# Decode attention and FFN over cached keys: the last batch's values in freed key slots, batches 0 to 6 finished while it loads

## The chip, the cores and the metric

The kernel runs on one core of one Trainium2 chip. The metric is the device time of one execution in microseconds (us); of several runs the median is taken.

The core has five engines with instruction queues of their own: TensorE (PE in the profile; PEld is its weight load), VectorE (DVE), ScalarE (ACT), GpSimd (POOL) and SyncE (SP). Here SP computes nothing: it issues all transfers (DMAs), in the order of its own instructions, and an issue that must wait for a semaphore holds up those behind it.

## The reference

Two layers of attention and two of a dense FFN, alternating, for 8 batches of one token each. Both attention layers read the same key and value caches and the same weights, and so do both FFN layers.

```
x: [8, 1, 512]   k_cache, v_cache: [8, 8, 8192, 128]   wq: [512, 4096]   wo: [4096, 512]
w1: [512, 1792]  w2: [1792, 512]    all bf16
def A(x):   q = (x @ wq) in 32 heads of 128; 4 heads share one of 8 key/value groups
            p = softmax(q . k / sqrt(128)) over 8192 keys;  o = p . v;  return o @ wo
def B(x):   return silu(x @ w1) @ w2
x = x + A(layernorm(x)); x = x + B(layernorm(x))
x = x + A(layernorm(x)); x = x + B(layernorm(x))
```

A batch's second attention needs its own first attention and first FFN; batches do not depend on each other. Each (batch, group) has 2 MB of keys and 2 MB of values, 256 MB in all.

## The kernel before, in words

A *unit* is (layer, batch, group): scores of 4 heads against 8192 keys, a softmax, and the product with the values. There are 128 units. Keys are loaded once for both layers: batch b's eight key blocks are kept in eight *slots* (`kts`, 2 MB each), turned in place by VectorE (L694, four transposes a block), used by layer 0 and later by layer 1. Values are loaded twice, once for each layer.

The work is cut in passes, `for b in range(-1, NB)`. Pass b holds layer 1 of batch b and layer 0 of batch b + 1, woven together by `pass_of`: a slot is given to batch b + 1's keys as soon as batch b's second use of it is scored (`scored[g]`). Pass -1 has only layer 0 of batch 0, pass 7 only layer 1 of batch 7. Between passes stands the turn: the output projection sum (`x2_node`), the FFN of one batch (`ffn_nodes`), a second norm, and the queries of groups 0 to 3 (`queries_0`, L642, weights resident). To have transfers to hide the turn, the value work of the last four layer-1 units of a pass is held back (`held`) and done after it: 16 single cells.

Values, wq's second half (`queries_1`, L665) and layer 0's wo pass through a *ring* of 7 cells of 512 KB. A load takes one cell or two neighbouring ones (`cells=1` or `2`), and waits on SP until the value product (L842) or projection that last read the cells is done. `values(h, wo, cells)` makes one unit's value work: loads, four value products of 8 matmuls each, then a high part by ScalarE (L852), a low part by VectorE (L856), a gather by TensorE (L864). In layer 0 the unit's wo block is loaded between its values (before the third quarter, or before the fourth with single cells) and multiplied at once (L915). In layer 1 the normed result goes to `qab` (L874).

In pass 7, wq's second half is asked for by the unit of group 4 (L1026), behind the values of groups 0 and 1, which are in the load order by then. All of wo for layer 1 is loaded once (`load_wo_all`, two loads of 2 MB to slots 0 and 2) after five units' values. At the end `out_proj_b` (L933) multiplies one group at a time for all 8 batches, then one FFN for all 8 (`ffn_nodes("e", big, 0, NB, ...)`: norm statistics L422, squares L436 and L440, six matmuls for each batch; the power L457 on GpSimd; up L492; tanh L498; gate L502; down L510), a turn to rows (L1058), a copy and the store.

The order on each engine is not written by hand. Every piece of work is a node with an engine, an estimated duration, a priority and its dependencies. `Plan.run` plays them through, with all loads strictly in the order in which they were made, and emits the instructions in the order in which that play started them. What it assumes: `RATE` us per MB of a load by its number of cells, `LAND` us from the end of a load's transfer to its use, a factor `PE_SLOW` on TensorE's durations. It also picks the ring cell of each load. These numbers set only the order and the cells; correctness comes from semaphores that `Sync` places.

Of the kernel before, what the change touches and what calls it, by code (L numbers as in the profile page):

```python
# [14 lines left out]
N_P = 3  # L15
# [120 lines left out]
class Plan:  # L136
# [4 lines left out]
    LAND = 2.0  # L141
    HOP = 0.1
    PE_SLOW = 1.15
# [107 lines left out]
def _build(ctx, nc, A_x, A_k_cache, A_v_cache, A_wq, A_wo, B_w1, B_w2, out):  # L251
# [68 lines left out]
    wsem = {n: DmaCounter(syn.new_sem(f"w_{n}")) for n in ("w1", "w2", "x", "wq0")}  # L320
# [89 lines left out]
    def norm_nodes(tag, prio, b0, nb, deps):  # L410
# [49 lines left out]
        def apply():  # L460
            if nb == 1:
                op(dve, lambda: dve.tensor_scalar(
                    xn[:, b0, :], xs[:, b0, :], nm, rstd[:, 0:1], op0=ALU.add, op1=ALU.mult),
                    reads=[res("xs"), res("misc"), res("rstd")], writes=[res("xn")])
            else:
                nmb = nm.unsqueeze(2).to_broadcast([128, nb, KT])
                rs = rstd[:, 0:nb].unsqueeze(2).to_broadcast([128, nb, KT])
                op(dve, lambda: dve.tensor_tensor(big_x, xs[:, bs, :], nmb, ALU.add),
                   reads=[res("xs"), res("misc")], writes=[res("ring", 1)])
                op(dve, lambda: dve.tensor_tensor(xn[:, bs, :], big_x, rs, ALU.mult),  # L470
                   reads=[res("ring", 1), res("rstd")], writes=[res("xn")])
# [9 lines left out]
    def ffn_nodes(tag, prio, b0, nb, deps):  # L481
# [3 lines left out]
        th, hs = (th1[:, :], hs1[:, :]) if nb == 1 else (big_th, big_hs)  # L485
# [212 lines left out]
    def keys(layer, b, g, q_dep, late=None, first=False):  # L698
# [5 lines left out]
        if late is None:  # L704
            sm = plain[0] % N_P
            plain[0] += 1
        else:
            sm = N_P + late
# [29 lines left out]
        for q in range(4):  # L738
# [11 lines left out]
            sn.append(plan.add(f"s{u}.{q}", "PE", 0.3, score, pr - 1,  # L750
# [68 lines left out]
    def values(h, wo=None, cells=2):  # L819

        layer, b, g, u, sm = h["layer"], h["b"], h["g"], h["u"], h["sm"]
        pr = count[0] - 1
# [5 lines left out]
        for P in range(4):  # L828
            if P == (2 if cells == 2 else 3) and wo is not None:
                h["wo"] = load_wo(wo)  # L830
            if P % cells == 0:
                vn = load_v(b, g, P, cells)

            def pv(P=P, vn=vn):


                vt = gran(vn.give, cells).rearrange("p (a c t n) -> p a c t n", a=cells, c=2, t=4)[:, P % cells]
                steps = []
                for c in range(2):
                    for t in range(4):  # L840
                        k = 32 * (2 * P + c) + 8 * t
                        steps.append(lambda t=t, c=c, k=k: pe.matmul(  # L842
                            ot[32 * t:32 * t + 2 * R, 0:2 * DH], pt[:, k:k + 2 * R], vt[:, c, t],
                            start=(P == 0 and c == 0), stop=(P == 3 and c == 1)))
                mms(steps, reads=cells_of(vn) + [res("p", sm)], writes=[res("ot", o)], add=(P > 0))
            n = plan.add(f"v{u}.{P}", "PE", 0.35, pv, pr, [h["exp"], vn, old or clear_n] + vs[-1:])
            if P % cells == cells - 1:
                frees(n, vn)
            vs.append(n)

# [73 lines left out]
    def out_proj_b(h, wn, prev):  # L924

        g = h["g"]

        def mul():
            w = slot(2 * (g // 4)).rearrange("p (h d) -> p h d", h=16)
            steps = []  # L930
            for r in range(R):
                for dt in range(KT):
                    steps.append(lambda r=r, dt=dt: pe.matmul(  # L933
                        YT[:, dt * NB:(dt + 1) * NB], w[:, R * (g % 4) + r, dt * 128:(dt + 1) * 128],
                        qab[:, :, R * g + r],
                        start=(g == 0 and r == 0 and dt == 0), stop=(g == G - 1 and r == R - 1),
                        skip_group_check=True))
            mms(steps, reads=[res("wo_all", g // 4)] + [res("attnb", g, b) for b in range(NB)],
                writes=[res("yt")], add=g > 0)
        return plan.add(f"e.w{g}", "PE", 0.56, mul, count[0] - 3, [h["n"], wn, prev])  # L940
# [25 lines left out]

    wo_all = []
    def load_wo_all():
        for i in range(2):
            n = plan.load(f"woall{i}", 4, None, scored[2 * i], ring=False)  # L970

            def emit(i=i):
                dma(sp, slot(2 * i).rearrange("p (h d) -> p h d", h=16), wo_v[:, 16 * i:16 * i + 16, :], ksem[2 * i],
                    writes=[res("kt", 2 * i), res("wo_all", i)])

            n.emit = emit
            wo_all.append(n)
# [19 lines left out]
    for b in range(-1, NB):  # L997
        ready = None
        prio = FIRST
        if b >= 0:  # L1000
# [5 lines left out]
            for h in held:  # L1006
                values(h, cells=1)
                ends.append(h)
        ks, vs, held_units = pass_of(b)
# [3 lines left out]
        def advance(unit):  # L1013
            while unit not in made:
                k = todo.pop(0)
                layer, kb, g = k
                if layer == 0:
# [4 lines left out]
                    if kb == 0 and g == 4:  # L1022
                        first_q.update(queries_1("f", count[0] - 5, 0, NB, [f5]))
                    made[k] = keys(0, kb, g, first_q[g])
                else:
                    if g == 4:  # L1026
                        second_q.update(queries_1(f"c{b}", count[0] - 3, b, 1, [ready]))
                    made[k] = keys(1, kb, g, second_q[g], held_units.index(k) if k in held_units else None, g == 0)

        for i, v in enumerate(vs):  # L1030
            advance(vs[min(i + (1 if i == 0 and b >= 0 else 2), len(vs) - 1)])
            if b == NB - 1 and i == 5:
                load_wo_all()
            if v[0] == 0:
                a_values(made[v], cells=1 if b >= 0 and i >= len(vs) - 3 else 2)
# [7 lines left out]

    w = free_yt[0]
    for h in ends[-G:]:
        w = out_proj_b(h, wo_all[h["g"] // 4], w)

    def e_x2():
        op(dve, lambda: dve.tensor_tensor(
            xs[:, :, :], YT[:, 0:KT * NB].rearrange("p (k b) -> p b k", b=NB), xs[:, :, :], ALU.add),  # L1050
            reads=[res("yt"), res("xs")], writes=[res("xs")])

    big = count[0] + 10
    n = plan.add("e.x2", "DVE", 0.2, e_x2, big, [w])
    n = ffn_nodes("e", big, 0, NB, [n])
# [54 lines left out]
```

## Time and profile before

| | |
|---|---|
| median of 5 runs | 1185.18 us (1183.28 to 1187.04) |
| profiled execution, its own time | 1187.04 us |
| its span, first to last instruction | 1185.3 us |
| mean granted TensorE clock | 0.67 |
| TensorE busy, VectorE busy | 709.1 us (60%), 596.8 us (50%) |
| ScalarE busy, GpSimd busy | 136.9 us (12%), 117.3 us (10%) |
| moved by DMA | 467.13 MB, mean 394 GB/s |
| SP waiting for value products (L842) | 653.8 us in 298 waits |
| SP waiting for scores (L746) | 156.4 us in 29 waits |

The page comes from one execution, the slowest of the five. Busy times are shares of the whole span. A table of windows gives the same by stretch: for each stretch its limits, its length, busy time and number of instructions of PE, PEld, DVE, ACT and POOL, the granted TensorE clock, the mean busy share of the 16 DMA engines and the GB/s moved. A timeline line gives the start, the duration, the engine, the line and the tiles, and in brackets how long the engine was idle before it and what ended that. A chain of waits gives a start, a length and what the end of the program hung on in that time.

### The profile page before, as it was taken

How to read it: one execution, taken by the hardware profiler on the slowest of the kernel's cores; microseconds unless marked ns; L12 is line 12 of the kernel's file. 1: busy time of each engine (PE TensorE's matmuls, PEld its weight loads, DVE VectorE, ACT ScalarE, POOL GpSimd, SP SyncE). 2: the span in 40 equal slices, each digit the busy share in tenths (PEclk: the TensorE clock that was granted, in tenths of full speed). 3: DMA queues.
4: the chain of work that ended last, by engine and by line, in shares of the span. 5: the costliest groups of instructions: out<-in, count | busy, mean ns of one | idle time of the engine just before them, and what ended most of it. 6: DMA issues, size and time to landing. Idle time of an engine off the chain costs nothing.

```text
span 1185.3 us, 31675 instructions
## 1 busy us (share of the span) xinstructions
PE 709.1 (60%) x13588; PEld 370.4 (31%) x13588; DVE 596.8 (50%) x1713; ACT 136.9 (12%) x475; POOL 117.3 (10%) x295
## 2 busy tenths in 40 slices
PE   2544555675565855656665756658556575566754
PEld 1222332342332423323332333324233242332433
DVE  5652367625565255733557245752557426563321
ACT  0010011111111110110111111111101111111110
POOL 1000011100110000100111000110101001110110
PEclk8565677656665576766767576775768667675775
DMA  9999799999999999999999999999999999999994
GB/s 364 422 420 347 310 421 420 411 404 400 415 412 378 404 374 415 425 405 386 419 423 408 407 400 415 413 406 398 411 406 414 406 382 422 408 399 389 384 349 174
DMA packets 86413, 467.13 MB, mean 394 GB/s; under 512 B 8944, under 2 KB 14848, under 8 KB 61952
## 3 DMA queue, kind: packets, MB, share of 16 engines
q1 hardware_dynamic: 86272, 465.10, 97.7%
q8 instruction: 107, 1.75, 0.6%
q14 instruction: 34, 0.28, 0.1%
HBM read 465.05 MB, written 0.01 MB: 392 GB/s over the span
## 4 chain that ended last, share of the span: by engine, by line
DMA 78%; PE 16%; issue 4%; DVE 1%; SPq 1%; POOLq 0%; ACT 0%; POOL 0%; DVEq 0%; ACTq 0%
DMA ring<-in_A_v_cache_dram 73%; PE ot L842 7%; PE sc L746 5%; DMA ring<-in_A_wq_dram 2%; DMA w<-in_B_w_dram 1%; DMA kts<-in_A_k_cache_dram 1%; PE misc L642 1%; SPq L340 1%; DVE kts L694 0%; PE ex L864 0%; PE sc L721 0%; PE yt L915 0%; PE misc L510 0%; DVE small L758 0%; PE ex L886 0%
## 5 line engine op out<-in xcount | busy, mean ns | idle before, releaser
L842 PE MATMUL ot<-ring,p 128*8 128x256 bf16 x4096 | 256.7, 364 | 223.0 <-DMA ring<-in_A_v_cache_dram 221.0
L694 DVE STREAM_TRANSPOSE kts<-kts 128x1024 uint32<-128x1024 uint32 x256 | 306.0, 1221 | 40.7 <-DMA kts<-in_A_k_cache_dram 40.6
L746 PE MATMUL sc<-kts,bd 128*32 128x256 bf16 x4096 | 288.3, 406 | 30.1 <-DVE kts L694 18.6
L842 PEld LDWEIGHTS ot<-ring,p 128*8 128x8 bf16 x4096 | 80.6, 92 | 316.6 <-DMA ring<-in_A_v_cache_dram 292.2
L746 PEld LDWEIGHTS sc<-kts,bd 128*32 128x32 bf16 x4096 | 115.0, 117 | 104.6 <-DVE kts L694 28.1
L856 DVE TENSOR_TENSOR part<-ot,p 128x256 bf16<-128x256 f32 x128 | 54.2, 424 | 171.2 <-ACT p L852 97.1
L763 POOL PARTITION_ALL_REDUCE small<-small x128 | 47.8, 373 | 640.4 <-DVE small L759 395.9
L772 ACT ACTIVATE expd<-sc,small 128x256 bf16<-128x256 f32 x128 | 60.7, 474 | 425.2 <-DVE small L767 376.5
L852 ACT ACTIVATE p<-ot 128x256 bf16<-128x256 f32 x128 | 49.0, 383 | 488.6 <-PE ot L842 487.6
L778 PE MATMUL sc<-expd,ident 128*32 128x256 bf16 x512 | 42.6, 322 | 91.5 <-ACT expd L772 88.0
L758 DVE TENSOR_REDUCE small<-sc 128x1 f32<-128x256 f32 x128 | 53.2, 416 | 54.4 <-PE sc L746 54.3
L792 POOL PARTITION_ALL_REDUCE small<-small x128 | 55.3, 432 | 217.6 <-DVE small L788 217.6
L729 DVE TENSOR_TENSOR bd<-sc,mask 128x64 bf16<-128x64 f32 x128 | 27.8, 217 | 82.9 <-PE sc L746 73.8
L785 DVE STREAM_TRANSPOSE p<-sc 128x256 bf16<-128x256 bf16 x128 | 56.9, 444 | 8.0 <-PE sc L778 5.9
L778 PEld LDWEIGHTS sc<-expd,ident 128*32 128x32 bf16 x512 | 15.3, 109 | 123.6 <-ACT expd L772 121.4
L788 DVE TENSOR_SCALAR small<-hm,small 128x4 f32<-128x4 f32 x128 | 26.4, 207 | 33.3 <-ACT expd L772 33.2
L864 PE MATMUL ex<-diag,p 128*128 128x4 bf16 x256 | 26.4, 172 | 23.8 <-DVE part L856 22.4
L915 PE MATMUL yt<-z,ring 128*128 128x4 bf16 x1024 | 36.1, 166 | 6.3 <-DVE z L893 4.7
L915 PEld LDWEIGHTS yt<-z,ring 128*128 128x128 bf16 x1024 | 31.3, 100 | 26.6 <-issue 25.9
L864 PEld LDWEIGHTS ex<-diag,p 128*128 128x128 bf16 x256 | 16.5, 105 | 72.9 <-issue 38.7
L767 DVE SCALAR_TENSOR_TENSOR small<-small,hm 128x4 f32<-128x4 f32 x128 | 19.4, 152 | 36.0 <-POOL small L763 36.0
L759 DVE TENSOR_SCALAR small<-hneg,small 128x4 f32<-128x4 f32 x128 | 29.4, 230 | 4.5
(82 smaller groups left out, 434.7 us busy)
## 6 DMA issues: line engine op xcount, KB each, us to landing
ring<-in_A_v_cache_dram SPq DMA_DIRECT2D x260, 512.0 KB, 8.2
kts<-in_A_k_cache_dram SPq DMA_DIRECT2D x64, 2048.0 KB, 11.4
ring<-in_A_v_cache_dram SPq DMA_DIRECT2D x126, 1024.0 KB, 11.0
ring<-in_A_wo_dram SPq DMA_DIRECT2D x64, 512.0 KB, 11.4
ring<-in_A_wq_dram SPq DMA_DIRECT2D x36, 512.0 KB, 9.8
kts<-in_A_wo_dram SPq DMA_DIRECT2D x2, 2048.0 KB, 15.6
w<-in_B_w_dram SPq DMA_DIRECT2D x2, 1792.0 KB, 14.2
wq<-in_A_wq_dram SPq DMA_DIRECT2D x4, 512.0 KB, 11.2
```

What stands on the lines that cost most here:

```text
L694: op(dve, lambda: dve.transpose(v, v), reads=[], writes=[res("kt", g)], add=(q > 0))
L746: steps.append(lambda t=t, y=y, w=w: pe.matmul(sc[32 * t:32 * t + 32, 0:256], w, kv[:, 2 * t + y, q], start=(q == 0 and y == 0), stop=(q = ...
L758: op(dve, lambda: dve.tensor_reduce(mxr[si], sv, AX.X, ALU.max), reads=[res(*scr)], writes=[res("mxr", si)])
L763: op(pool, lambda: pool.partition_all_reduce(mxa[si], mxp[si], 128, bass.bass_isa.ReduceOp.max), reads=[res("mxp", si)], writes=[res("mxa" ...
L772: op(act, lambda: act.activation(pe_out[:, :], sv, ACT.Exp, bias=bias[si], scale=SM_SCALE, accum_out=rsum[si]), reads=[res(*scr), res("bia ...
L778: steps = [lambda P=P: pe.matmul(sc[32 * P:32 * P + 32, 256:512], src[:, P], pe_out[:, :], start=True, stop=True) for P in range(4)]
L785: op(dve, lambda: dve.transpose(pt[:, :], src), reads=[res(*scr)], writes=[res("p", sm)])
L792: op(pool, lambda: pool.partition_all_reduce(ssa[si], ssm[si], 128, bass.bass_isa.ReduceOp.add), reads=[res("mxp", si)], writes=[res("mxa" ...
L842: steps.append(lambda t=t, c=c, k=k: pe.matmul(ot[32 * t:32 * t + 2 * R, 0:2 * DH], pt[:, k:k + 2 * R], vt[:, c, t], start=(P == 0 and c = ...
L852: op(act, lambda: act.activation(pt[:, :], ot[:, 0:2 * DH], ACT.Copy), reads=[res("ot", o)], writes=[res("p", sm)])
L856: op(dve, lambda: dve.tensor_tensor(part[:, :], ot[:, 0:2 * DH], pt[:, :], ALU.subtract), reads=[res("ot", o), res("p", sm)], writes=[res( ...
L915: steps.append(lambda j=j, dt=dt: pe.matmul(YT[:, dt * R:(dt + 1) * R], w[:, j, dt * 128:(dt + 1) * 128], zt[:, R * j:R * j + R], start=(g ...
```

## The change

Six edits:

1. The last batch's pass is taken out of the loop and written out. wq's second half is asked for right behind the held values of batch 6. The keys' work of groups 0 to 6 is made at once, each with a buffer of its own for its probabilities (`buf`); group 7 uses group 0's again, after its values. Groups 0 and 1 load values through the ring in single cells, groups 2 to 7 into key slots 0, 1, 2, 5, 6, 7 by `load_v_slot`, each when the slot is scored; group 7's in three loads of 2, 1 and 1 quarters. wo goes to slots 3 and 4, between group 4's and group 5's values.
2. The second output projection, residual sum and FFN are made twice: for batches 0 to 6 ("d") while the last batch loads, and for batch 7 alone ("e") at the end. Scratch tiles are cut to the number of batches.
3. Layer 0's wo block is loaded behind all of its unit's values.
4. The last three layer-0 units of pass -1 also load single cells, as those of the other passes do.
5. The planner's numbers: `LAND` 2.0 to 5.0, `PE_SLOW` 1.15 to 1.0, a score node 0.3 to 0.45, a value node 0.35 to 0.4.
6. `queries_1` also depends on the copy of the first half's queries; three more semaphores.

```diff
-    LAND = 2.0
+    LAND = 5.0
...
-    PE_SLOW = 1.15
+    PE_SLOW = 1.0
...
+    def load_v_slot(b, g, k):
+        parts = (2, 1, 1) if g == G - 1 else (4,)
+        src = A_v_cache[b, g].rearrange("(p y) d -> p (y d)", p=128)
+        got = []
+        for i, cells in enumerate(parts):
+            q = sum(parts[:i])
+            where = res("vs", k, i)
+
+            def emit(i=i, q=q, cells=cells, where=where):
+                dma(sp, slot(k)[:, GR * q:GR * (q + cells)], src[:, GR * q:GR * (q + cells)],
+                    ksem[k] if len(parts) == 1 else wsem[f"end{i}"],
+                    writes=[where] + ([res("kt", k)] if i == 0 else []))
+
+            n = plan.load(f"v{b}.{g}.{q}", cells, emit, scored[k], ring=False)
+            got += [(n, slot(k)[:, GR * (q + j):GR * (q + j + 1)], where) for j in range(cells)]
+        return got
...
-        pr = count[0] - 1
+        pr = count[0] - 1 if b < NB - 1 else u + 1
+        quarters = load_v_slot(b, g, at) if at is not None else None
...
-            if P == (2 if cells == 2 else 3) and wo is not None:
-                h["wo"] = load_wo(wo)
-            if P % cells == 0:
+            if quarters:
+                vn = quarters[P][0]
+            elif P % cells == 0:
                 vn = load_v(b, g, P, cells)
...
+        if wo is not None:
+            h["wo"] = load_wo(wo)
...
-                a_values(made[v], cells=1 if b >= 0 and i >= len(vs) - 3 else 2)
+                a_values(made[v], cells=1 if i >= len(vs) - 3 else 2)
...
+    fin = NB - 1
+    second_q.update(queries_1(f"c{fin}", FIRST + 6, fin, 1, [ready, second_q[3]]))
+    made = [keys(1, fin, g, second_q[g], first=g == 0, buf=g % (N_P + N_DEF)) for g in range(G - 1)]
+    values(made[0], cells=1)
+    made.append(keys(1, fin, G - 1, second_q[G - 1], buf=0))
+    values(made[1], cells=1)
+    for g, k in ((2, 0), (3, 1), (4, 2)):
+        values(made[g], at=k)
+    load_wo_all()
+    for g, k in ((5, 5), (6, 6), (7, 7)):
+        values(made[g], at=k)
     w = free_yt[0]
-    for h in ends[-G:]:
-        w = out_proj_b(h, wo_all[h["g"] // 4], w)
+    done = [h["n"] for h in ends] + [made[1]["n"]]
+    for g in range(G):
+        w = out_proj_b("d", g, 0, fin, [w, wo_all[g // 4]] + done)
+    n = x2_of("d", 0, fin, count[0] + 20, [w])
+    fed = ffn_nodes("d", count[0] + 20, 0, fin, [n, second_q[G - 1]])
+    w = n
+    for g in range(G):
+        w = out_proj_b("e", g, fin, 1, [made[g]["n"], w])
     big = count[0] + 10
-    n = plan.add("e.x2", "DVE", 0.2, e_x2, big, [w])
-    n = ffn_nodes("e", big, 0, NB, [n])
+    n = x2_of("e", fin, 1, big, [w])
+    n = ffn_nodes("e", big, fin, 1, [n, fed])
```

## The prediction

> **What bounds the kernel now.** I read the page first: the DMA row of its second part and the GB/s row under it.
>
> ```profile
> DMA  9999799999999999999999999999999999999994
> GB/s 364 422 420 347 310 421 420 411 404 400 415 412 378 404 374 415 425 405 386 419 423 408 407 400 415 413 406 398 411 406 414 406 382 422 408 399 389 384 349 174
> ```
>
> Thirty-eight slices of forty are full; TensorE is busy 60%, VectorE 50%. The kernel streams 467.13 MB, and both kernels read the same tensors once. Nothing on an engine counts unless it empties the DMA queues or lies after the last transfer. So the next view is the table of windows, 4 us each, over the places that are not full (the last two columns are DMA share and GB/s).
>
> ```profile
> 88.00:92.00 4.00, 1.03 (x16) 0.38 (x16) 4.00 (x4) 0.00 (x0) 0.00 (x0) 0.55 0.84 347
> 92.00:96.00 4.00, 3.01 (x48) 1.33 (x48) 1.06 (x4) 0.38 (x1) 0.33 (x1) 0.60 0.95 337
> 96.00:100.00 4.00, 1.88 (x48) 1.26 (x48) 1.27 (x8) 0.74 (x3) 0.47 (x2) 0.83 0.87 306
> 100.00:104.00 4.00, 1.27 (x20) 0.57 (x20) 0.42 (x1) 0.39 (x2) 0.00 (x0) 0.50 0.89 330
> ...
> 124.00:128.00 4.00, 3.63 (x96) 2.84 (x100) 0.61 (x4) 0.00 (x0) 0.00 (x0) 0.50 0.03 11
> 128.00:132.00 4.00, 2.98 (x56) 1.26 (x44) 1.81 (x10) 0.57 (x2) 0.83 (x2) 0.83 0.59 168
> ...
> 1124.00:1128.00 4.00, 2.99 (x68) 2.02 (x72) 0.50 (x3) 0.00 (x0) 0.00 (x0) 0.50 0.85 295
> 1128.00:1132.00 4.00, 3.67 (x80) 2.19 (x72) 1.19 (x6) 0.67 (x3) 0.37 (x1) 0.82 0.49 141
> ...
> 1168.00:1172.00 4.00, 2.23 (x44) 0.99 (x40) 0.42 (x1) 0.38 (x1) 0.00 (x0) 0.50 0.10 41
> ```
>
> Four holes: the end of the first pass (88 to 104), the turn after it (120 to 132), the last pass (1124 to 1132), and everything after about 1168. In between, seven windows of 140 us show shares of 1.00 to 1.02.
>
> What makes the third hole, from the chain of waits:
>
> ```profile
> 1115.29 9.84 DMA ring<-in_A_wq_dram
> 1125.17 0.60 PE misc L665 x16
> ...
> 1126.61 1.09 PE sc L746 x16
> ```
>
> The second half of wq, needed for heads groups 4 to 7 of the last batch, is asked for only behind the values of units 0 and 1. Units 4 to 7 cannot be scored before 1126, so the ring cells holding their values are not freed, and the SP queue waits. What follows the last landing, from the timeline:
>
> ```profile
> 1170.00 1.03 PE L842 MATMUL ot<-ring,p 128*8 128x256 bf16 x16 [0.80 <-DMA ring<-in_A_v_cache_dram]
> 1173.26 0.19 DVE L1049 TENSOR_TENSOR xs<-yt,xs 128x32 bf16<-128x32 f32 x1 [0.69 <-PE yt L933]
> 1175.91 1.69 POOL L457 TENSOR_TENSOR rstd<-var,expo 128x8 f32<-128x8 f32 x1 [33.20 <-DVE ring L468]
> 1177.95 1.65 PE L492 MATMUL misc<-xn,w 128*128 128x8 bf16 x56 [2.74 <-DVE xn L470]
> ```
>
> From 1170.00 to the span's end at 1185.3 it is a serial tail of 15.3 us, without transfers.
>
> **What the skill says.** The Trainium skill, "DMA: Bandwidth & Descriptors", section "Anatomy of one DMA", says that a DMA's fixed cost is mostly the wait for the last byte's receipt, about 2 us, and that waits are held on the issuing sequencer while the DMA engines just eat their queues. The trace agrees: the share ends about 0.4 us into 1168 to 1172 (0.10 of 4 us), and TensorE starts on the last values at 1170.00, 1.6 us later. So a blocked load on SP holds every load behind it. The section "Where 436 GB/s comes from" gives a ceiling of 435 GB/s; the full passes run at 402 to 412, so the steady part has little left in it. "TensorE: Matmul & The Clock Gate", Part 1, says that the clock is half until a window of about 3.4 us was busy. The records show 0.50 from 1143 to the end, through bursts of matmuls: I price TensorE's work in the tail at half clock.
>
> **The change, part by part.** The sum is made against the profiled execution, 1187.04 us (span 1185.3 and 1.7 around it). That is the highest of five, 1.9 above the median; the savings are then taken off the median.
>
> *Last batch, wq early.* wq's four cells now stand right behind the 16 held cells, before the values of units 0 and 1. Units 4 to 7 can be scored some 8 cells earlier. One 1.27 us step a cell (the four L665 groups start at 1121.38, 1122.66, 1123.94, 1125.17) makes 10 us, so unit 4's queries come at about 1116, while units 2 and 3 are scored (their L758 at 1115.50 and 1118.19). TensorE then scores units 4 to 7 at some 2.5 us each, ready by about 1128.
>
> *Values in freed slots.* Units 2 to 7 load into key slots. These loads wait on SP for the score of their own slot, not for a ring cell freed by a softmax and a value product. Behind a waiting one stand all later loads, wo too. The order is units 2, 3, 4 (slots 0 to 2), wo (slots 3, 4), units 5, 6, 7. The first three slots are scored before 1116; slot 7 is wanted only after about 27 us of queued loads (three at 5.0 and two of wo at 6.0, from the L933 groups at 1148.81 and 1154.81), so it is a dozen us early. No wait is left. Third hole gone: (1 - 0.85) x 4 + (1 - 0.49) x 4 = **2.64 us**. Bounds: 1.5 if TensorE's queue, which now has value products waiting for cells among the scores, holds some of it; 2.9 with the small dips beside it.
>
> *Single cells and wo last in pass -1.* Windows 88 to 104 miss (0.16 + 0.05 + 0.13 + 0.11) x 4 = 1.8 us. The SP row there shows pair loads at 95.35 and 102.70, each waiting for two neighbouring cells. Single cells go out as each falls free. But the last keys' four transposes (4.63 us from 87.58) still hold the first part. I take half, **0.9 us**; bounds 0 and 1.8. The second hole stays: it is the chain from w2's landing at 120.18 through down projection, norm, queries and first score to 128.8, and none of it is touched.
>
> *Passes 0 to 6: wo behind the values, new planner constants.* The load order changes only in wo's place, which is held less long: it is used after the unit's last values. The dips of a fast pass (428 to 440: shares 0.92, 0.80, 0.97, so 1.2 us; 964 to 968: 0.88, so 0.5) come to some 2 us in the seven. LAND, PE_SLOW and the new durations move value products and scores against each other in TensorE's order; in the turn of a pass nine single-cell products stand between the last output projection and the first query matmul, before and after. I take **1.0 us** gained; the bounds are 2 us gained and, as nothing in the trace shows the new order, about 9 lost (rival 3).
>
> *Size of loads.* Six pairs become twelve singles in pass -1, ten pairs become five quads, and the last unit gets one pair and two singles. At the planner's own 2.57, 2.51, 2.48 us per MB (an estimate from its table): 6 x 0.06 - 10 x 0.03 + 0.06, about **0.1 us** lost.
>
> *The tail.* Only batch 7 is left in it. In the first turn the same chain for one batch ran freely: L963 at 113.99, L492 at 116.34, 2.35 us. Now L1049 to L492 takes 1177.95 - 1173.26 = 4.69. Gain 2.34: 42 fewer square matmuls, one var operation for three, and the power at 0.58 (mean of 16) for 1.69. Tanh 0.18 for 0.27 and gate 0.17 for 0.27 add 0.19; **2.5 us** in all. The up and down projections cost 1.65 either way.
>
> Against it stands the work for batches 0 to 6, now inside the stream. Counted from the last landing as 0: unit 5 lands near -10.1, unit 6 at -5.1, the last unit at -2.5, -1.3, 0. From -10.1 TensorE has, at half clock, 12 value products of 0.53 (1162.26 to 1162.79), four of them after -2.5; four projections of 0.53 (1162.79 to 1163.32), up and down for seven batches at 1.6 each, a gather of 0.1. That is 6.4 + 2.1 + 3.2 + 0.1 = 11.8 us, so the last product ends at +1.7, not at +0.6 as eight free matmuls would. Now it ends at +1.03. So **0.65 us** is lost; bounds: a gain of 0.4 at full clock, a loss of 2 if the wo of slots 3 and 4 comes late and everything queued behind its wait slips. What follows (ACT, DVE, gather, norm) is unchanged, as unit 6's projection fits into the 1.1 us before the last gather. Tail: -1.9.
>
> Sum: -2.64 - 0.9 - 1.0 + 0.1 - 1.9 = **-6.3 us**. Against its own execution 1187.04 gives 1180.7; off the median 1185.18 gives **1178.8**.
>
> **Rivals.** (1) *The stream gains more.* All dips go (1.8 and 2), the clock is full in the tail (+1.1): -2.9 - 1.8 - 2 - 3.0 makes about -9.7, 1175.5, and more if fewer waiting loads lift the 402 to 412 GB/s. For: a freed queue is never empty in the last 45 us. Against: shares of 1.01 leave nothing to fill. (2) *Given back at the end.* The hole is filled, but TensorE falls behind by 3 us instead of 0.65, and pass -1 gains nothing: -2.64 - 2.5 + 3 = about -2, 1183. For: half clock, and products, projections and FFN in one queue. Against: the next landing is known and late. (3) *Slower.* In passes 0 to 6 the planner, which now believes in landings 3 us later and a faster TensorE, puts value products behind scores that are not ready; ring cells fall free late, and each of seven passes gets one more dip like 428 to 440, 1.24 us. That is +8.7 with no gain there: 1178.8 + 1.0 + 8.7 = 1188.5. It decides from about 0.8 us a pass. For: the whole order moves, and 7 cells last only 9 us. Against: DMA shares show slack, with landings 8.2 us (median) after issue.
>
> **Numbers.** Forecast (1176 to 1183) 0.56, rival 1 0.18, rival 2 0.14, rival 3 0.12. The range must leave out no more than 2 in 10: 1173.0 covers most of rival 1, 1186.0 all of rival 2. A change under 0.2% (2.4 us) can't be told from none: same is 1182.8 to 1187.6. Faster takes the forecast, rival 1 and a little of rival 2: 0.75; same 0.13; slower 0.12.
>
> **What would show it.** Windows at full share from 1120 to the last landing; no wait of SP longer than a few us there except at its end; last landing near 1165.5; tail near 13.4 us with the last product about 1.7 after the landing; the first turn's hole as before. It is wrong if passes 0 to 6 differ by over 2 us, or if TensorE's products trail the landings.

## The result, and the profile after

| | before | changed |
|---|---|---|
| median of runs | 1185.25 us (78 runs, 1179.01 to 1192.93) | 1180.86 us (41 runs, 1174.66 to 1188.11) |
| ratio to before, 95% interval | | 0.9961 [0.9949, 0.9973] |
| profiled execution, its span | 1187.04, 1185.3 us | 1179.38, 1177.7 us |
| granted TensorE clock | 0.670 | 0.661 |
| last landing; from there to the end of the span | 1169.95; 15.37 us | 1162.30; 15.36 us |

The change is faster by 4.6 us (3.2 to 6.0 by the interval). The two profiled executions lie 7.6 us apart, because that of before was a long one and that of the changed kernel a short one for its kernel. Landings are taken from the trace's records of when each load's last increment arrived.

The DMA rows of the changed kernel's page, in 40 slices of the span, look like those of before:

```profile
DMA  9999799999999999999999999999999999999993
GB/s 364 422 418 397 317 418 418 412 379 418 419 414 405 399 421 404 415 376 389 413 401 408 402 392 420 422 400 394 413 406 411 398 379 420 419 415 403 396 394 156
```

The fourth slice, the end of the first pass, is at 397 GB/s and was at 347; the others differ in both directions. The table of windows of the changed kernel shows the places that the prediction worked on, and the end (length; busy time of PE, PEld, DVE, ACT, POOL; clock; DMA share; GB/s):

```profile
88.00:92.00 4.00, 1.59 (x24) 0.32 (x24) 3.92 (x4) 0.00 (x0) 0.00 (x0) 0.61 1.03 410
92.00:96.00 4.00, 3.42 (x56) 1.57 (x56) 1.16 (x4) 0.56 (x2) 0.00 (x0) 0.54 1.03 407
96.00:100.00 4.00, 2.14 (x48) 1.08 (x48) 1.41 (x7) 0.95 (x3) 0.80 (x2) 0.89 1.03 410
100.00:104.00 4.00, 2.29 (x44) 1.16 (x48) 0.34 (x2) 0.17 (x1) 0.00 (x0) 0.50 1.03 410
...
120.00:124.00 4.00, 3.66 (x96) 2.84 (x100) 0.59 (x4) 0.00 (x0) 0.00 (x0) 0.50 0.04 15
124.00:128.00 4.00, 3.00 (x56) 1.31 (x44) 1.84 (x10) 0.57 (x2) 0.83 (x2) 0.70 0.57 180
...
1124.00:1128.00 4.00, 3.35 (x76) 1.87 (x72) 1.89 (x11) 1.13 (x4) 1.23 (x3) 1.00 1.04 438
1128.00:1132.00 4.00, 2.19 (x62) 1.25 (x52) 2.08 (x10) 1.17 (x4) 0.81 (x3) 1.00 0.96 401
...
1156.00:1160.00 4.00, 3.24 (x92) 2.30 (x90) 0.61 (x2) 0.38 (x1) 0.29 (x1) 0.50 0.73 292
1160.00:1164.00 4.00, 4.00 (x113) 2.90 (x113) 0.60 (x3) 0.25 (x1) 0.00 (x0) 0.50 0.10 36
1164.00:1168.00 4.00, 3.48 (x79) 2.27 (x68) 1.17 (x4) 0.77 (x2) 0.00 (x0) 0.50 0.01 4
```

The reader is to see that 88 to 104 is now wholly full; that the turn's hole comes one window earlier but is as long; that the hole at 1124 to 1132 is gone; and that TensorE is busy without a gap from 1160 to 1164, where hardly anything is transferred any more. The last is where the expected gain in the tail went. TensorE's timeline of the changed kernel there (start, duration, engine, line, tiles; in brackets the idle time before it and what ended that):

```profile
1151.59 0.24 PE L436 MATMUL misc<-xd,xs 128*128 128x1 bf16 x4
1153.71 0.19 PE L440 MATMUL misc<-cst 128*128 128x1 bf16 x2 [1.87 <-issue]
...
1153.99 0.60 PE L869 MATMUL ot<-kts,p 128*8 128x256 bf16 x8
...
1157.66 1.23 PE L492 MATMUL misc<-xn,w 128*128 128x7 bf16 x40
1159.65 0.57 PE L492 MATMUL misc<-xn,w 128*128 128x7 bf16 x16 [0.76 <-issue]
...
1161.83 1.65 PE L510 MATMUL misc<-ring,w 128*128 128x7 bf16 x56
1163.41 2.73 PE L869 MATMUL ot<-kts,p 128*8 128x256 bf16 x48
...
1170.51 1.65 PE L492 MATMUL misc<-xn,w 128*128 128x1 bf16 x56 [1.42 <-DVE xn L462]
```

The 48 matmuls at 1163.41 are unit 6's last two and all four of unit 7's value products, 8 matmuls each. Not one of them waits for a landing: all data is there at 1162.30, but the down projection of batches 0 to 6 (1161.83) and a row of things before it stand ahead. They end at 1166.14, 3.84 us after the last landing; in the kernel before it was 1.08. Two idle stretches are marked "issue": TensorE stood still for 1.87 and 0.76 us with nothing in the profile that it waited for.

### The profile page after: what moved, and what is told of

Same layout as the page of the kernel before. It is cut to its first block, busy times and chain, and to the rows that moved or that the text cites. A ratio compares the mean times of both kernels' runs of the same rounds, so it can differ in the third digit from the quotient of the medians.

```text
span 1177.7 us, 32198 instructions
## 1 busy us (share of the span) xinstructions
PE 718.8 (61%) x13836; PEld 372.7 (32%) x13836; DVE 596.6 (51%) x1718; ACT 138.4 (12%) x477; POOL 117.7 (10%) x296
## 4 chain that ended last, share of the span: by engine, by line
DMA 67%; PE 20%; DVE 6%; issue 4%; ACT 1%; SPq 1%; POOL 1%; POOLq 0%; DVEq 0%; ACTq 0%
DMA ring<-in_A_v_cache_dram 60%; PE sc L748 8%; PE ot L869 6%; DMA kts<-in_A_wo_dram 2%; DMA ring<-in_A_wq_dram 2%; DVE kts L694 2%; DMA w<-in_B_w_dram 1%; PE misc L642 1%; PE yt L944 1%; SPq L340 1%; PE ex L893 1%; DVE small L760 1%; ACT expd L774 1%; DVE part L885 1%; ACT p L881 1%
## 5 line engine op out<-in xcount | busy, mean ns | idle before, releaser
L869 PE MATMUL ot<-ring,p 128*8 128x256 bf16 x3904 | 239.9, 359 | 198.6 <-DMA ring<-in_A_v_cache_dram 196.1
L748 PE MATMUL sc<-kts,bd 128*32 128x256 bf16 x4096 | 293.5, 405 | 22.0 <-DVE kts L694 12.6
L869 PEld LDWEIGHTS ot<-ring,p 128*8 128x8 bf16 x3904 | 76.2, 92 | 292.5 <-DMA ring<-in_A_v_cache_dram 269.6
L748 PEld LDWEIGHTS sc<-kts,bd 128*32 128x32 bf16 x4096 | 107.3, 115 | 87.1 <-DVE bd L731 22.2
L885 DVE TENSOR_TENSOR part<-ot,p 128x256 bf16<-128x256 f32 x128 | 53.0, 414 | 120.6 <-ACT p L881 70.0
L922 DVE TENSOR_TENSOR z<-ex,rc 128x16 bf16<-128x16 f32 x64 | 11.1, 174 | 69.4 <-PE ex L915 69.4
## 6 DMA issues: line engine op xcount, KB each, us to landing
kts<-in_A_v_cache_dram SPq DMA_DIRECT2D x5, 2048.0 KB, 16.6
```

The source lines that it names most:

```text
L748: steps.append(lambda t=t, y=y, w=w: pe.matmul(sc[32 * t:32 * t + 32, 0:256], w, kv[:, 2 * t + y, q], start=(q == 0 and y == 0), stop=(q = ...
L869: steps.append(lambda t=t, c=c, k=k: pe.matmul(ot[32 * t:32 * t + 2 * R, 0:2 * DH], pt[:, k:k + 2 * R], vt[:, c, t], start=(P == 0 and c = ...
L885: op(dve, lambda: dve.tensor_tensor(part[:, :], ot[:, 0:2 * DH], pt[:, :], ALU.subtract), reads=[res("ot", o), res("p", sm)], writes=[res( ...
```

## Where the time went, by stretch

The bytes that the loads have moved mark the same point of the work in each kernel. Times are from each kernel's profiled executions, two of each (the second ones are the experiments before_again and after_again); the cut points are when the transfers of 10% and of 90% of all bytes had begun. The stretch from the last landing to the end of the span is called the tail.

| stretch | before | changed | difference of the means | prediction's steps |
|---|---|---|---|---|
| start to 10% of bytes (pass -1) | 120.1, 120.1 | 116.5, 116.2 | -3.75 | -0.9 |
| 10% to 90% (passes between) | 925.4, 926.6 | 926.1, 928.2 | +1.15 | -1.0 |
| 90% to last landing (last pass) | 124.4, 121.5 | 119.7, 119.9 | -3.2 | -2.64 |
| last landing to end (tail) | 15.37, 15.38 | 15.36, 15.13 | -0.1 | -1.9 |
| span | 1185.3, 1183.6 | 1177.7, 1179.4 | -5.9 | -6.3, with 0.1 lost by load sizes |

The sum comes near the one predicted, but from other places: pass -1 gives four times as much, the tail nothing.

One line of this table says less than it seems. The changed kernel and two of the experiments below, no_split and wo_early, differ only in the last pass. Their traces show the same loads in the same order, and the same work in the same order on every engine (by tiles and shapes), from the start to 1113 us at least. Yet from 10% to 90% of the bytes the changed kernel's two executions took 926.1 and 928.2 us, that of no_split 922.5 and that of wo_early 931.0. So this stretch differs by up to 8.5 us from one execution to another with the order unchanged, and a difference of a few us in it, in single executions, says nothing of a kernel's order. The totals scatter likewise: 1174.66 to 1188.11 us over the runs of the changed kernel. Pass -1, the last pass and the tail are steadier: each agrees within 0.3 us in the two executions of the changed kernel, though the last pass of before took 124.4 and 121.5.

## Experiments

Each ratio is to the kernel before, run beside it on the same chip. "First hole" is the time after 110 us at which fewer than 3 of the 16 DMA engines first move data.

| kernel | median, runs | ratio [95%] | first hole | 10 to 90% | 90% to landing | tail |
|---|---|---|---|---|---|---|
| last_only | 1178.21, 9 | 0.9945 [0.9922, 0.9969] | 123.0 | 924.1 | 119.2 | 13.94 |
| const_only | 1179.36, 19 | 0.9958 [0.9938, 0.9978] | 124.5 | 920.8 | 121.0 | 15.37 |
| order_only | 1180.49, 22 | 0.9969 [0.9955, 0.9983] | 120.6 | 928.3 | 124.5 | 15.37 |
| no_split | 1178.91, 12 | 0.9964 [0.9949, 0.9978] | 120.2 | 922.5 | 119.7 | 14.73 |
| singles_only | 1184.38, 22 | 0.9994 [0.9978, 1.0009] | 121.5 | 930.7 | 120.9 | 15.38 |
| wo_last_only | 1184.18, 14 | 0.9984 [0.9964, 1.0004] | 122.2 | 925.1 | 121.9 | 15.38 |
| wo_early | 1181.05, 22 | 0.9950 [0.9931, 0.9968] | 120.2 | 931.0 | 121.1 | 13.04 |
| best_old | 1177.89, 6 | 0.9937 [0.9912, 0.9962] | 120.5 | 928.5 | 119.8 | 12.22 |
| best_old_again | 1178.04, 7 | 0.9937 [0.9907, 0.9967] | 120.1 | 928.7 | 120.8 | 12.23 |
| best_mid | 1174.17, 6 | 0.9899 [0.9870, 0.9927] | 120.1 | 925.5 | 119.3 | 12.25 |
| before_again | 1185.20, 14 | 0.9993 [0.9971, 1.0014] | 124.4 | 926.6 | 121.5 | 15.38 |
| after_again | 1181.25, 22 | 0.9957 [0.9940, 0.9975] | 120.0 | 928.2 | 119.9 | 15.13 |

Before and changed stand at 124.2 and 120.5 for the first hole. The stretches and the tail are those of each kernel's one profiled execution.

The last pass (90% to landing) can be compared over all executions. In the six of kernels that load its values through the ring (before, before_again, const_only, order_only, singles_only, wo_last_only) it took 120.9 to 124.5 us, 122.4 in the mean; in the eight with values in key slots 119.2 to 121.1, 119.9 in the mean. That is 2.4 us, near the prediction's 2.64, though the two ranges touch.

### The change taken apart: last_only, const_only, order_only, no_split

*last_only* is the changed kernel with edits 3, 4 and 5 undone: only the last batch's own pass is left.

```diff
-    LAND = 5.0
+    LAND = 2.0
...
-    PE_SLOW = 1.0
+    PE_SLOW = 1.15
...
+            if P == (2 if cells == 2 else 3) and wo is not None:
+                h["wo"] = load_wo(wo)
...
-        if wo is not None:
-            h["wo"] = load_wo(wo)
...
-                a_values(made[v], cells=1 if i >= len(vs) - 3 else 2)
+                a_values(made[v], cells=1 if b >= 0 and i >= len(vs) - 3 else 2)
```

> The changed kernel with three edits taken back: the planner's numbers, the place of layer 0's wo block, the pairs in the first pass. What is left is the last batch's own pass. Theory A (the gain lies in the last pass): the hole of 2.6 us is gone, the tail stays near 15.3 us because TensorE is behind; ratio to the kernel before 0.998 (about -2.6 us), and the hole between the first passes starts at 122.7 us as before. Theory B (the gain comes from the planner's order in the earlier passes): ratio 1.000.

The ratio was 0.9945, not worse than the whole change and a larger gain than either theory had. The first hole stays late (123.0), the last pass is short (119.2), and the tail is 13.94 us, where some 15.3 was expected. Its last product ended 2.04 us after the landing at 1162.55. TensorE's timeline of last_only:

```profile
1160.72 0.24 PE L492 MATMUL misc<-xn,w 128*128 128x7 bf16 x3 [0.97 <-issue]
...
1164.20 0.39 PE L871 MATMUL ot<-kts,p 128*8 128x256 bf16 x8
...
1164.64 1.55 PE L510 MATMUL misc<-ring,w 128*128 128x7 bf16 x56
```

Here the last products stand before the down projection of batches 0 to 6, in the changed kernel behind it. That is part of the tail's loss. Edits 3 and 4 touch layer 0 alone, so this order is put down to the planner's numbers (edit 5); no run changed these alone here.

*const_only* is the kernel before with the planner's numbers alone (edit 5).

```diff
-    LAND = 2.0
+    LAND = 5.0
...
-    PE_SLOW = 1.15
+    PE_SLOW = 1.0
...
-            sn.append(plan.add(f"s{u}.{q}", "PE", 0.3, score, pr - 1,
+            sn.append(plan.add(f"s{u}.{q}", "PE", 0.45, score, pr - 1,
...
-            n = plan.add(f"v{u}.{P}", "PE", 0.35, pv, pr, [h["exp"], vn, old or clear_n] + vs[-1:])
+            n = plan.add(f"v{u}.{P}", "PE", 0.4, pv, pr, [h["exp"], vn, old or clear_n] + vs[-1:])
```

> The kernel before with the planner's numbers alone (landing 5.0, TensorE factor 1.0, score node 0.45, value node 0.4). Theory A: within 1 us of the kernel before, ratio 0.9992 to 1.0008, hole of the last pass still 2.6 us or smaller by under 1 us. Theory B: most of the measured gain of 4.4 us, ratio about 0.997.

These numbers, for which the prediction had a place in a term of 1.0 us, bring 0.9958 alone, as much as the whole change. The table of windows of const_only over the place of the third hole:

```profile
1124.00:1128.00 4.00, 3.89 (x88) 2.14 (x84) 2.14 (x12) 1.09 (x4) 1.09 (x3) 1.00 1.00 406
1128.00:1132.00 4.00, 4.00 (x88) 1.98 (x80) 2.43 (x12) 1.37 (x5) 1.01 (x3) 1.00 0.98 352
```

By the shares the hole is gone here too, though wq still stands behind the values of units 0 and 1. That the numbers filled it is not shown: singles_only, wo_last_only and order_only, which leave the last pass's loads in their old order, have no such hole either (shares of 0.94 or more from 1124 to 1132). Nor does the stretch from 90% to the landing, 121.0 us, differ clearly from the 121.5 of before_again. The passes between were some 5 us shorter in this execution, which is within the scatter of that stretch. So the gain of 5 us stands in the 19 runs, but the trace doesn't place it.

*order_only* is the kernel before with wo behind the values and single cells at the end of pass -1 (edits 3 and 4).

```diff
-            if P == (2 if cells == 2 else 3) and wo is not None:
-                h["wo"] = load_wo(wo)
...
+        if wo is not None:
+            h["wo"] = load_wo(wo)
...
-                a_values(made[v], cells=1 if b >= 0 and i >= len(vs) - 3 else 2)
+                a_values(made[v], cells=1 if i >= len(vs) - 3 else 2)
```

> The kernel before with the order of loads alone: wo behind its unit's values, single cells at the end of the first pass. Theory A: the stalls of 88 to 104 us (1.8 us of DMA share) are gone, so that the next hole starts up to 3.5 us earlier as in the changed kernel; ratio 0.998 (about -2 us). Theory B: ratio 1.000, the hole starts where it did.

0.9969, or 3.7 us, with the first hole at 120.6: the whole gain of pass -1 comes from these two edits. The last pass (124.5, before 124.4 and 121.5) and the tail (15.37) are not shortened.

last_only (edits 1, 2 and 6), const_only (5) and order_only (3 and 4) together hold every edit once. Alone they gain 6.5, 5.0 and 3.7 us by their ratios, 15 in all, and the whole change 4.6: the gains don't add.

*no_split* is the changed kernel with one output projection and one FFN for all eight batches at the end (edit 2 undone; the projection's priority is set for its new place).

```diff
-        return plan.add(f"{tag}.w{g}", "PE", 0.56, mul, count[0] + (20 if nb > 1 else 0), deps)
+        return plan.add(f"{tag}.w{g}", "PE", 0.56, mul, count[0], deps)
...
-        w = out_proj_b("d", g, 0, fin, [w, wo_all[g // 4]] + done)
-    n = x2_of("d", 0, fin, count[0] + 20, [w])
-    fed = ffn_nodes("d", count[0] + 20, 0, fin, [n, second_q[G - 1]])
-    w = n
-    for g in range(G):
-        w = out_proj_b("e", g, fin, 1, [made[g]["n"], w])
+        w = out_proj_b("e", g, 0, NB, [w, wo_all[g // 4], made[g]["n"]] + done)
     big = count[0] + 10
-    n = x2_of("e", fin, 1, big, [w])
-    n = ffn_nodes("e", big, fin, 1, [n, fed])
+    n = x2_of("e", 0, NB, big, [w])
+    n = ffn_nodes("e", big, 0, NB, [n])
```

> The changed kernel with the second output projection and FFN made once for all 8 batches at the end, as before. If the split hides work (as I forecast, tail near 13.4 us), taking it back costs about 2 us: tail above 15 us, last product within 1 us of the last landing, ratio to before about 0.998. If TensorE's backlog eats what the split saves (the changed kernel's trace: last product 3.8 us behind the last landing), it costs nothing: ratio about 0.996, as the changed kernel.

Its ratio, 0.9964, is not different from the changed kernel's 0.9961: finishing seven batches early, as it is placed in the change, is worth nothing within the intervals (0.0015, or 1.8 us, to each side). In the traced executions the tail is even shorter without it, 14.73 us against 15.36 and 15.13. TensorE's timeline of no_split shows why:

```profile
1158.65 0.39 PE L869 MATMUL ot<-kts,p 128*8 128x256 bf16 x8 [0.32 <-DMA kts<-in_A_v_cache_dram]
...
1165.96 1.66 PE L492 MATMUL misc<-xn,w 128*128 128x8 bf16 x56 [2.74 <-DVE xn L470]
```

Without the early work TensorE waits for the last landing (1158.61) and its last product ends 0.43 us after it; the long chain for eight batches follows. In the changed kernel the short chain follows, but 3.84 us after the landing.

### Which edit fills pass -1: singles_only, wo_last_only

Each is the kernel before with one line of order_only's diff: single cells for the last three units of pass -1, or wo behind its unit's values.

```diff
-                a_values(made[v], cells=1 if b >= 0 and i >= len(vs) - 3 else 2)
+                a_values(made[v], cells=1 if i >= len(vs) - 3 else 2)
```

> The kernel before with single cells for the last three layer-0 units of pass -1, and nothing else. Theory (pairs of cells at the end of pass -1 hold the queue): most of the 3.6 us by which order_only's first turn hole starts earlier, the hole from about 121.0 to 127, windows 88 to 104 at full share; ratio 0.997. Rival (wo between the values holds the queue): hole starts at 123.5 or later, ratio 0.999 to 1.000. Last pass hole and tail (15.4 us) as before by both.

> The kernel before with layer 0's wo block loaded behind all of its unit's values, and nothing else. Theory (single cells make the gain in pass -1): the first turn's hole starts within 1 us of before (123 to 124.5), ratio 0.999 to 1.000. Rival (wo between the values was what held the queue): the hole starts at about 121, ratio 0.997. Last pass hole and tail (15.4 us) as before by both; a window of 140 us in the middle passes differs by under 1 per cent.

The table of windows of singles_only:

```profile
88.00:92.00 4.00, 1.24 (x20) 0.25 (x24) 3.92 (x4) 0.00 (x0) 0.00 (x0) 0.50 1.02 409
92.00:96.00 4.00, 3.17 (x56) 1.17 (x56) 1.25 (x3) 0.38 (x1) 0.00 (x0) 0.71 1.03 411
96.00:100.00 4.00, 2.54 (x56) 1.36 (x48) 1.65 (x9) 0.63 (x3) 0.80 (x2) 0.72 1.02 405
100.00:104.00 4.00, 2.16 (x33) 0.70 (x34) 0.60 (x2) 0.56 (x2) 0.00 (x0) 0.50 1.02 408
```

and of wo_last_only:

```profile
88.00:92.00 4.00, 1.02 (x16) 0.38 (x16) 4.00 (x4) 0.00 (x0) 0.00 (x0) 0.50 0.86 356
92.00:96.00 4.00, 3.02 (x52) 1.80 (x52) 1.23 (x3) 0.43 (x2) 0.00 (x0) 0.50 0.87 322
96.00:100.00 4.00, 2.00 (x44) 1.19 (x44) 1.74 (x9) 0.69 (x3) 0.80 (x2) 0.80 0.97 386
100.00:104.00 4.00, 1.77 (x44) 1.27 (x48) 0.60 (x2) 0.56 (x2) 0.00 (x0) 0.63 1.01 405
```

Single cells fill all four windows and bring 10% of the bytes to 117.0; wo behind the values fills the second half and brings them to 118.4 (before 120.1, both 116.5). Both help and the gains overlap; neither of my two stories had it so. Single cells count for more at this place. In the total neither can be told from no change (intervals from 0.998 to 1.001 and 0.996 to 1.000). In singles_only's execution the passes between took 930.7 us against 926.0 (the mean of before's two), which hides the 3.1 us won before them; it is again within the scatter of that stretch. Why its 22 runs don't show the gain stays open. The two profiled executions lie 1.3 us above and 1.4 below their kernels' medians, so their parts can't be set against the ratios closely.

### Is the backlog at the end the cause: wo_early, best_old, best_mid

wo_early is the changed kernel with the second layer's wo in slots 0 and 1, right behind group 1's values, so that the work for batches 0 to 6 can start earlier.

```diff
-    WO_AT = (3, 4)
+    WO_AT = (0, 1)
...
-    for g, k in ((2, 0), (3, 1), (4, 2)):
-        values(made[g], at=k)
     load_wo_all()
-    for g, k in ((5, 5), (6, 6), (7, 7)):
-        values(made[g], at=k)
+    for g in range(2, G):
+        values(made[g], at=g)
```

> The changed kernel with one thing moved: wo of the second layer goes to slots 0 and 1, right behind the values of group 1, and groups 2 to 7 each load their values into their own slot. The projections and the FFN of batches 0 to 6 can then start some 15 us earlier. Theory (TensorE's backlog from this work lies just before the last values and costs the tail): the last value product ends within 2.0 us of the last landing instead of 3.8, the tail is 12.3 to 13.5 us instead of 15.36, ratio to before about 0.994 (0.002 under the changed kernel). Rival (the tail is late because the sixteen DMA engines drift apart and the last landings come bunched): tail stays at 15 us or more and the last product 3 us or more behind the landing, ratio as the changed kernel's, 0.996. No hole in the last pass by either.

best_old is wo_early with the planner's old numbers and the first layer's wo between the values as before (edits 5 and 3 undone, by the lines shown under last_only); best_mid is wo_early with the old numbers only.

> As wo_early, but with the planner's old numbers (LAND 2.0, PE_SLOW 1.15, 0.3 and 0.35) and layer 0's wo loaded between its unit's values as in the kernel before; single cells at the end of pass -1 kept. Theory: the planner's new numbers are not needed, as the early values in freed slots remove the last pass's hole alone; first turn's hole starts where singles put it, tail 12.3 to 13.5 us, ratio 0.993 to 0.995. Rival (new numbers carry a gain of their own in the passes between): ratio 0.997 or more, with windows of 140 us in the middle passes below 402 GB/s.

> The changed kernel with wo in slots 0 and 1 right behind the values of group 1 (as in wo_early) and the planner's old numbers, and wo of layer 0 behind its unit's values (kept). Theory (order edits of pass -1, values in slots and early wo each carry their part): tail 12.2 to 13.1 us, hole of the first turn as early as in the changed kernel, ratio 0.9925 to 0.994. Rival (old numbers with wo last load the passes worse): ratio 0.996 or more.

> best_old a second time, for the time of the best version so far and for its tail: theory (the early wo takes the backlog off the end in every execution): last value product within 1.5 us of the last landing, tail 12.2 to 13.1 us, ratio 0.9925 to 0.995. Rival (its 12.22 us was luck): tail over 14 us, ratio 0.996 or more.

The tail fell to 13.04 us in wo_early and to 12.22, 12.23 and 12.25 in the others. TensorE's timeline of best_mid:

```profile
1137.79 0.24 PE L436 MATMUL misc<-xd,xs 128*128 128x1 bf16 x4
...
1143.93 1.66 PE L510 MATMUL misc<-ring,w 128*128 128x7 bf16 x56
...
1158.55 1.02 PE L869 MATMUL ot<-kts,p 128*8 128x256 bf16 x16 [0.60 <-DMA kts<-in_A_v_cache_dram]
...
1161.02 0.60 PE L869 MATMUL ot<-kts,p 128*8 128x256 bf16 x8
...
1166.03 1.65 PE L492 MATMUL misc<-xn,w 128*128 128x1 bf16 x56 [1.42 <-DVE xn L462]
```

The down projection of the seven batches runs at 1143.93, 17 us before the last landing at 1160.98. The value products wait for their landings again, and the last ends 0.64 us after the last one. The clean comparison is wo_early, where the place of wo and of what hangs on it is all that was moved: the same products, the same FFN and the same chain for one batch, with the last product 1.46 us after the landing instead of 3.84 and 3.61, and a tail of 13.04 us. So the lost tail is the backlog. The rival, landings that come bunched, fails: in wo_early the 16 DMA engines finished the last load 5.55 us apart, further than in the changed kernel (3.95 and 3.27), and the last product still followed the landing closely.

wo_early's total did not clearly follow: 0.9950 can't be told apart from 0.9961. In its traced execution the passes between took 931.0 us, and the table of windows, 140 us each, has two low ones:

```profile
560.00:700.00 140.00, 85.86 (x1608) 42.84 (x1604) 72.35 (x210) 16.65 (x58) 13.98 (x34) 0.66 1.00 394
...
840.00:980.00 140.00, 86.91 (x1636) 43.84 (x1636) 69.89 (x209) 16.93 (x59) 13.99 (x34) 0.66 1.00 396
```

In best_mid the same two stand at 409 and 407 GB/s. But in no_split, whose order up to there is that of wo_early, they stand at 403 and 405, so the low windows don't belong to the order. best_mid's ratio, 0.9899 [0.9870, 0.9927], lies below wo_early's interval and the changed kernel's, over six runs: with the early wo the new planner numbers lose some 6 us, though by themselves (const_only) they gained. The runs show this; where those 6 us lie, no trace does. I had expected 0.9925 to 0.994. best_mid is the fastest version found, about 7 us faster than the changed kernel.

### The same kernels again: before_again, after_again

> The kernel before, unchanged, profiled a second time and timed against itself. Theory (the hole of the last pass at 1124 to 1132 belongs to the kernel's order): a stretch of 8 us near there is again at shares of 0.85 and 0.49 or lower, 2 us or more missing, last landing after 1168. Rival (it came from how the loads' landings fell in that one execution, since two kernels that touch nothing after pass -1 did not show it): under 1.0 us missing between 1112 and 1140, last landing 1167 or earlier. The ratio to itself shows what the measurement can tell: 1.000 with an interval of about 0.002 to each side. Tail 15.4 us by both.

> The changed kernel, unchanged, profiled a second time. Theory (TensorE's backlog at the end belongs to its order): the last value product again ends 3 us or more behind the last landing, tail 14.8 to 15.8 us. Rival (accident of that execution): under 2.5 us behind, tail under 14 us. First turn's hole starts at 118 to 119.5 in the windows' sense (share under 0.1 in 120 to 124) by both. Ratio 0.996.

The table of windows of before_again:

```profile
1120.00:1124.00 4.00, 2.14 (x54) 1.63 (x52) 1.15 (x5) 0.17 (x2) 0.43 (x1) 0.55 1.03 416
1124.00:1128.00 4.00, 3.52 (x64) 1.89 (x68) 0.59 (x3) 0.00 (x0) 0.00 (x0) 0.60 0.59 240
1128.00:1132.00 4.00, 3.77 (x76) 2.09 (x74) 2.32 (x11) 0.95 (x3) 0.80 (x2) 1.00 0.93 320
```

The hole is there again, 1.92 us by the shares of its two windows, where the first execution missed 2.64. So it is no accident of one execution. But singles_only, wo_last_only and order_only don't have it, though they leave the last pass's loads in their old order and only shift the ring cells and TensorE's order there (wo_last_only and order_only move wo in the passes between as well), and order_only took 124.5 us from 90% to the landing without it. The late wq is therefore not enough to make this hole, and the hole is not all that lengthens the last pass. In after_again the last product again ends 3.6 us after the landing at 1164.25, with idle stretches marked "issue" of 1.50 and 1.03 us at the same two places.

## Why the prediction was right, and where not

The predicted time was 1178.8, the measured one 1180.86, inside the range and on the forecast's side. That they lie so near is in part luck: pass -1 gave 2.9 us more than forecast and the tail 1.8 less, and these errors largely cancel. By its own steps:

- *Last batch, wq early and values in freed slots, -2.64.* Right in effect: no hole in 1124 to 1132, and -3.2 over the stretch (-2.4 between the means of all executions with and without values in slots). As the account of one hole it is not shown: four kernels with wq as late as before lack that hole too.
- *Single cells and wo last in pass -1, -0.9.* The mechanism was right, the term four times too small. Two causes. I read the missing time from the DMA share (1.8 us), which counts the time that packets took, whatever they moved. The GB/s column of the same four lines sums to 1320 against four times the 410 that a full window moves there: 320 x 4 us is 1280 KB, or 3.1 us; the next window (340 GB/s, after the change 401) has another 0.6. That is the 3.7 measured. And I halved it, because the last keys' transposes would hold the first part; singles_only shows full windows beside the same transposes (3.92 us of VectorE in 88 to 92).
- *The second hole stays.* Right: 124.2 to 129.8 became 120.5 to 125.8.
- *Passes 0 to 6, -1.0.* +1.15 between the two pairs of executions, far inside the scatter of this stretch (8.5 us with one and the same order), so neither the sign nor the size is settled. Rival 3, nine us lost, did not come. That the planner's numbers can be worth several us is shown by ratios alone: const_only gains 5.0, and wo_early stands 6 us behind best_mid.
- *Size of loads, +0.1.* Too small to be measured.
- *The tail, -1.9.* This is the step that failed. Its gain was right: from the end of the last product to the span's end it is 11.52 us now and was 14.29, so 2.77 against the 2.5 forecast. Its loss was mis-sized: "the last product ends at +1.7" was +3.84, so 2.76 us were lost and not 0.65. The working counted 11.8 us of queued work from unit 5's landing. That landing came at 1152.40, 9.9 us before the last, but unit 5's first product started at 1153.99, held for 1.59 us, nearly all of it the stall in the norm's small matmuls; the second stall added 0.76. These 2.35 us are the difference of 2.14, within what the rounded durations leave. The loss lies beyond the bound of 2 that the prediction kept for it, and near rival 2's "3 us" behind; that it did not make the 1183 of that rival is due to pass -1. The prediction's own sign of being wrong, products that trail the landings, came true.
- *A reading beside the sum.* The prediction took the end of the transfers from the share of 0.10 in 1168 to 1172, found 1.6 us from there to TensorE's start, and called this agreement with the "about 2 us" of the Trainium skill, "DMA: Bandwidth & Descriptors", section "Anatomy of one DMA". A mean share doesn't say when the last engine ends. By the packet records the last packet before the landing ended at 1169.52, 0.43 us before the landing at 1169.95; in all fourteen executions it is 0.28 to 0.55 us. The trace does not agree with a wait of 2 us there. The skill's section is about transfers that GpSimd issues, and these loads are issued by SP. No term rests on it.

That the tail's backlog sets the loss is shown by moving it (wo_early, and again best_old and best_mid). That the two stalls make up its excess is read from the timeline; no run took them away alone. Why the new planner numbers help alone and hurt with the early wo stays open, as does what makes executions of one order differ by more than the change is worth.

## What to carry to other kernels

To hide the epilogue of earlier work beside a stream, put it so early in the stream that its engine is idle again when the last data lands. Work that "fits" into the last ten microseconds leaves no room for a stall, and here gave the whole gain back. Read a part-empty DMA window from its bytes against those of a full window, not from the busy share. When two edits remove the same wait, measure each alone before adding their gains. And before a difference between two traces is put down to an edit, look how far two traces with the same order lie apart in that stretch.

## What the runs showed of the hardware

**TensorE stopped without a wait.** The stalls of 1.87 and 0.76 us (changed kernel), 1.50 and 1.03 (after_again), 0.94 and 0.97 (last_only) fall in or after long rows of short matmuls. The view of the DMA queues of the changed kernel in the window 1151 to 1154 has one packet that is no data:

```profile
q1 hardware_dynamic: 100, 1.22, 96.8%
q8 instruction: 1, 0.02, 2.2%
```

From 1146 to 1151 and from 1154 to 1157 there is none; 1157 to 1160 has the next. By the trace's records each is 16,384 bytes and takes 1.06 to 1.11 us at these places, and TensorE went on 1.2 to 1.5 us after its end, in all six stalls. The Trainium skill, "Runtime: NRT & Kernel Launch", section "Instruction fetch mechanics", says that each sequencer fetches its instructions in 16 KiB blocks of 256 over a DMA queue of its own while it executes, and that this is mostly hidden. The size agrees, and by their number the packets are TensorE's: 109 of them beside 27,987 records of TensorE instructions in the changed kernel, 107 beside 27,491 in no_split and 27,452 in before, one for each 257. "Hidden" agrees for most of them, but not in these places. In all fourteen traces TensorE stood idle for over 0.4 us with "issue" as the reason twelve times, and each time it went on 1.2 to 1.6 us after the end of such a packet. That ties the stalls to the fetching; no run changed the fetching, so the cause isn't isolated.

**A deep queue ends raggedly.** The trace has 16 reports for each load, and the landing is the last of them. For the last load the first and the last report lay 1.61 and 1.27 us apart in the two executions of before, 3.95 and 3.27 in those of the changed kernel, 5.55 in wo_early. Over all traces it was 1.1 to 2.9 us in the six with ring values and 3.1 to 5.6 in the eight with values in slots. It shows in the windows above: 0.73, then 0.10 of the engines busy. In the kernels with values in slots the loads wait in the queue longer: in the changed kernel 16.6 us in the median from issue to landing for five 2 MB value loads, where the 1 MB pairs of before took 11.0. That this is the reason is not shown, as the last load's size differs too (1 MB in the ring, 512 KB in the slots), and what it costs was not tried.
